# A planned kernel of two attentions: V projected in three parts, VectorE's scores in a third bank, and new planner settings

## The chip, the cores and the metric

The kernel runs on one core of a Trainium2 chip. The engines of the core work side by side and wait for each other by semaphores: TensorE (PE in the profile, PEld for its weight loads), VectorE (DVE), ScalarE (ACT), GpSimd (POOL) and SyncE (SP), which issues nearly all transfers here. The metric is the device time of one execution in microseconds; lower is better.

## The reference

Two attentions over the same input `x` (2048 tokens, 640 features, bf16), mixed by a gate per token:

```python
x = A_x
g = _sigmoid((x * gate_w).sum(-1, keepdims=True))
a = _A_ref(x, A_wqkv, A_wo)
b = _B_ref(x, B_wqkv, B_wo)
return g * a + (1 - g) * b
```

Both have 32 heads of 20 features. A is full softmax attention, every query with all 2048 keys:

```python
scores = jnp.einsum("bhqd,bhkd->bhqk", q, k) * scale
p = _softmax(scores, axis=-1)
o = jnp.einsum("bhqk,bhkd->bhqd", p, v)
return (...)(o).reshape(B, S, D) @ wo
```

B lets each query see 8 keys, at the distances 0, 2, ... 14 before it (positions before the start are masked), with the same softmax, sum over V and output projection.

## The kernel before

**Tiling.** A's work is cut into 32 groups: 4 blocks of 512 queries (`qc`) by 8 sets of 4 heads (`q`), in the order of `GROUPS`. A group has 64 units: 16 blocks of 128 keys (`kb`) by 4 heads (`j`). A unit is one matmul of scores, 128 keys by 512 queries, with the 20 features of a head in one quarter of the array's rows, so up to four units of different `j` run at once. Its exponential and a matmul with V (21 columns: a column of ones gives the sum of the softmax) follow; the four heads of a group accumulate in the four column quarters of `obank`.

**Two ways to the exponential.** Most units go through ScalarE: a tile is two or three units whose scores fill two or three PSUM banks of `score[s % 2]`, and one ACTIVATE (L1652) takes 1024 or 1536 columns to bf16 in `ebuf`. Other units go through VectorE in quads (one `kb`, four `j`). Such a unit "rides" with a tile: its scores are written by the same score matmuls (`qk`, L1616 to L1647), and VectorE turns them into bf16 bit patterns with an add and a max (L1642, into `uD`). Each quad is then used four times with shifted exponents (L866 adds the shift, GpSimd scales V in L857, and the sums go into `obank` in L1693).

**Banks.** Three PSUM banks are shared: `side[0]` is a bank of its own, and `side[1]` and `side[2]` are the third banks of the two score buffers. Side work takes them: the projections of Q, K and V (`mm_group`, L577, matmuls on L592), the gate, B's attention and the output projections. A tile can have three units, or two and a ride, only if the third bank `x` of its own score buffer is free; otherwise it has two units.

**Order.** The order of all engines is fixed when the program is built. A planner keeps a clock for each engine, adds a charge for every task (`T`), and works through the tiles. `next_tile` (L1577) picks the units and asks `wanted` (L1505) for a ride; `qk`, `exp` and `pv_slot` place scores, exponential and sums; then `spend` lets side work run until a limit, the planned end of the exponential before plus `SLACK`. Side work is a set of generators with priorities. A generator yields what it wants next: `("bank", need)` for a shared bank, `("pe", charge, ready)`, `("dve", ...)`, or `("cond",)` and `("cond2", time)` to wait; `step` (L1226) decides whether it gets it. PE works strictly in the planned order, so a matmul that waits holds up all later ones, scores too. `filler` (L1700, matmuls on L1714) adds matmuls whose result isn't used where the planned load of PE is below `FILL`.

**Settings.** `PLAN` (L50) holds a tuple of 21 settings per entry and the tile number from which it holds: slacks, tolerances for a bank that is nearly free (`XTOL`), priorities, limits on VectorE's lag and on quads, and others (list on L1806).

**Projections.** `gen_v(half)` (L762) projects V in two halves of 320 columns, that is 16 heads: a block of 128 tokens in one bank, 20 column-tiled matmuls, one copy by VectorE (L773) into `vA`. The first block of the first half is `v_first` and `v_out` (L1372, L1380), before the first scores; the other fifteen follow from the start (priority 1), and the second half begins with the second group. `gen_kd` (L620) projects K in five chunks, the next when the group in `KPACE` is reached. `gen_qd` (L689) projects Q per chunk and query block (bank, matmuls, copy to `dst` in L706), moves it into `qT` with DMAs (L709), takes absolute values (L715), multiplies by `KMd` in a further bank (L729; this gives a bound for the exponent), and sends the bound, `qbnd`, into `qT` too (L749). B's weights are rearranged by 15 copies on GpSimd (L884, `gen_bweights`). `gen_b` has small matmuls of 64 columns (L996 and L1006) in its middle.

Of the kernel before, what the change touches and what calls it, by code (L numbers as in the profile page):

```python
# [14 lines left out]
P = 128  # L15
# [20 lines left out]
POS = {c: g for g, c in enumerate(GROUPS)}  # L36

# [13 lines left out]
    0: ((0.3, 0.64), 0.39, 2.5, 2.5, 0.49, -1.3, -0.1, 11.8, 7.0, 7.2, 0.49, 0.47, 4.4, 4.0, 0.0, 0.75, 2, -3, 0.36, 4.0, 3.0),  # L51
    10: ((0.3, 0.64), 0.32, 2.5, 2.5, 0.45, -1.3, -0.1, 13.26, 7.0, 7.2, 0.49, 0.68, 4.4, 4.0, 0.0, 0.6, 2, 0.0, 0.5, 4.0, 4.0),
    20: ((0.3, 0.64), 0.32, 2.5, 2.5, 0.45, -1.3, -0.1, 13.26, 7.0, 7.2, 0.35, 0.68, 4.4, 4.0, 0.0, 0.6, 2, 0.0, 0.5, 4.0, 3.0),
    30: ((0.3, 0.49), 0.54, 2.5, 2.5, 0.45, -1.26, -0.1, 13.26, 6.2, 7.2, 0.35, 0.68, 4.4, 4.23, 0.0, 0.6, 2, 0.0, 0.5, 4.0, 3.0),
    40: ((0.3, 0.49), 0.54, 2.5, 2.5, 0.45, -1.32, -0.1, 13.26, 6.2, 7.2, 0.35, 0.66, 4.4, 4.23, 0.0, 0.6, 2, 0.0, 0.5, 4.0, 2.0),
    50: ((0.3, 0.52), 0.54, 2.5, 2.5, 0.67, -1.26, -0.28, 13.26, 6.2, 8.47, 0.35, 0.68, 4.4, 4.23, 0.0, 0.71, 2, -3, 0.5, 4.0, 3.0),
    70: ((0.35, 0.49), 0.54, 2.5, 2.5, 0.97, -1.6, -0.28, 12.22, 6.2, 7.47, 0.17, 0.7, 3.98, 3.89, -0.1, 0.7, 2, -3, 0.5, 4.0, 3.0),
    80: ((0.35, 0.49), 0.54, 2.5, 2.5, 0.97, -1.6, -0.28, 12.22, 6.2, 7.47, 0.17, 0.7, 3.98, 3.89, -0.08, 0.7, 2, -3, 0.5, 4.0, 3.0),
    90: ((0.35, 0.49), 0.54, 2.5, 2.5, 0.97, -1.09, -0.28, 12.22, 6.2, 7.47, 0.17, 0.7, 3.98, 3.89, -0.08, 0.63, 2, -3, 0.5, 4.0, 3.0),
    100: ((0.41, 0.49), 0.61, 2.5, 2.5, 1.07, -1.09, -0.28, 11.68, 6.2, 7.47, 0.17, 0.7, 2.76, 3.89, -0.08, 0.59, 2, -3, 0.5, 4.0, 4.0),  # L60
    110: ((0.32, 0.49), 0.5, 2.5, 2.5, 0.92, -0.82, -0.28, 15.02, 6.2, 9.99, 0.17, 0.7, 2.14, 3.89, -0.08, 0.68, 2, -3, 0.44, 4.0, 4.0),
    120: ((0.28, 0.49), 0.54, 2.5, 2.5, 0.97, -1.6, -0.28, 12.22, 6.2, 7.47, 0.17, 0.7, 3.98, 3.71, -0.03, 0.7, 2, -3, 0.5, 4.0, 3.0),
    140: ((0.32, 0.49), 0.5, 2.5, 2.5, 0.92, -0.82, -0.28, 15.02, 6.2, 9.99, 0.19, 0.7, 2.14, 3.89, -0.08, 0.68, 2, -3, 0.44, 4.0, 4.0),
    150: ((0.32, 0.49), 0.5, 2.5, 2.5, 0.92, -0.71, -0.28, 15.73, 6.2, 10.9, 0.19, 0.64, 2.14, 3.89, 0.02, 0.68, 2, -3, 0.44, 4.0, 4.0),
    170: ((0.3, 0.64), 0.32, 6.6, 2.5, 0.49, -1.3, -0.1, 9.4, 7.0, 7.2, 0.52, 0.47, 4.46, 4.0, 0.0, 0.9, 2, 0.0, 0.5, 4.0, 3.0),
    180: ((0.3, 0.64), 0.32, 6.6, 2.5, 0.66, -1.3, -0.1, 9.4, 7.0, 7.2, 0.52, 0.47, 4.46, 4.0, 0.0, 0.9, 2, 0.0, 0.5, 4.0, 3.0),
    190: ((0.3, 0.64), 0.32, 6.6, 2.5, 0.66, -1.3, -0.1, 9.4, 4.5, 7.2, 0.52, 0.47, 4.46, 4.0, 0.0, 0.9, 2, 0.0, 0.5, 4.0, 3.0),
    200: ((0.3, 0.64), 0.32, 6.6, 2.5, 0.66, -1.3, -0.1, 9.4, 5.5, 7.2, 0.52, 0.48, 4.46, 4.0, 0.0, 0.9, 2, 0.0, 0.5, 4.0, 3.0),
    210: ((0.3, 0.64), 0.32, 6.6, 2.5, 0.63, -1.6, -0.1, 9.4, 5.5, 7.2, 0.5, 0.48, 4.35, 4.0, 0.0, 0.88, 2, 0.0, 0.5, 4.0, 3.0),
    220: ((0.3, 0.64), 0.32, 6.6, 2.5, 0.49, -1.3, -0.1, 11.8, 7.0, 7.2, 0.48, 0.47, 4.4, 4.0, 0.0, 0.6, 2, 0.0, 0.5, 4.0, 3.0),  # L70
    230: ((0.28, 0.49), 0.54, 2.5, 1.0, 0.97, -1.6, -0.28, 12.22, 6.2, 7.47, 0.17, 0.7, 3.98, 3.34, 0.04, 0.7, 2, -3, 0.5, 4.0, 3.0),
    240: ((0.3, 0.47), 0.54, 2.5, 2.5, 0.67, -1.26, -0.28, 13.26, 6.2, 8.47, 0.35, 0.68, 4.4, 4.23, 0.0, 0.71, 2, -3, 0.5, 4.0, 3.0),
    250: ((0.3, 0.47), 0.54, 2.5, 2.5, 0.67, -1.26, -0.28, 13.26, 6.2, 8.47, 0.35, 0.68, 4.4, 4.23, 0.0, 0.71, 2, -3, 0.41, 4.0, 3.0),
    260: ((0.3, 0.47), 0.54, 2.5, 2.5, 0.67, -1.26, -0.28, 13.26, 6.2, 8.47, 0.39, 0.68, 4.4, 4.23, 0.0, 0.71, 2, -3, 0.17, 4.0, 3.0),
    270: ((0.3, 0.55), 0.54, 2.5, 2.5, 0.67, -1.26, -0.23, 13.26, 6.7, 8.77, 0.39, 0.72, 4.4, 4.23, -0.17, 0.71, 2, -3, 0.17, 4.0, 3.0),
    280: ((0.3, 0.64), 0.32, 6.6, 2.5, 0.49, -1.5, -0.1, 11.8, 1.0, 7.2, 0.48, 0.47, 4.4, 4.0, 0.0, 0.6, 2, 0.0, 0.5, 4.0, 3.0),
    290: ((0.3, 0.64), 0.28, 6.6, 6.6, 0.49, -1.5, -0.1, 11.8, 6.7, 7.2, 0.48, 0.46, 4.4, 4.0, 0.0, 0.6, 2, 0.0, 0.5, 4.0, 3.0),
    300: ((0.3, 0.47), 0.54, 2.5, 2.5, 0.6, -1.05, -0.28, 12.11, 6.2, 8.47, 0.39, 0.62, 4.4, 4.23, 0.0, 0.71, 1, -3, 0.17, 4.0, 3.0),
    310: ((0.3, 0.38), 0.54, 2.5, 2.5, 0.6, -1.05, -0.28, 12.11, 6.2, 8.47, 0.39, 0.62, 4.4, 4.23, 0.0, 0.71, 1, -3, 0.17, 4.0, 3.0),
    340: ((0.25, 0.64), 0.32, 6.6, 2.5, 0.66, -1.3, -0.06, 10.84, 4.5, 5.62, 0.52, 0.7, 4.46, 3.26, 0.0, 0.9, 2, 1, 0.52, 4.0, 3.0),  # L80
    350: ((0.3, 0.64), 0.23, 5.5, 2.5, 0.71, -1.07, -0.1, 8.63, 4.5, 7.2, 0.52, 0.48, 4.21, 4.0, 0.0, 0.9, 2, 0.0, 0.35, 4.0, 3.0),
    360: ((0.3, 0.64), 0.23, 6.6, 2.5, 0.71, -1.07, -0.1, 8.63, 4.5, 7.2, 0.52, 0.48, 4.21, 4.0, 0.0, 0.9, 2, 0.0, 0.35, 4.0, 2.0),
    380: ((0.3, 0.64), 0.23, 6.6, 2.5, 0.71, -1.07, -0.1, 8.63, 4.5, 7.2, 0.61, 0.48, 4.21, 4.0, 0.0, 0.9, 2, 0.0, 0.35, 4.0, 2.0),
    390: ((0.3, 0.64), 0.23, 6.6, 2.5, 0.71, -1.07, -0.1, 8.63, 4.5, 7.2, 0.61, 0.48, 4.21, 4.0, 0.0, 0.73, 2, 0.0, 0.35, 4.0, 2.0),
    400: ((0.3, 0.64), 0.23, 6.6, 2.5, 0.71, -1.07, -0.1, 8.63, 4.5, 7.2, 0.61, 0.48, 4.61, 4.0, 0.0, 0.7, 2, 0.0, 0.35, 4.0, 2.0),
    410: ((0.3, 0.64), 0.23, 6.6, 2.5, 0.6, -1.07, -0.1, 8.63, 4.5, 7.2, 0.61, 0.48, 4.61, 4.0, 0.07, 0.7, 2, 0.0, 0.35, 4.0, 2.0),
# [1803 lines left out]
```

## Time and profile before

| | us |
|---|---|
| median of 3 runs | 802.85 (802.61 to 802.86) |
| profiled execution, its time | 802.24 |
| its span, first to last instruction | 800.4 |
| TensorE busy in it | 770.4 |
| ScalarE busy | 779.5 |
| VectorE busy | 717.6 |
| GpSimd busy | 143.6 |
| DMA, mean rate over the span | 44 GB/s |

The granted TensorE clock was 1.00 throughout. "Busy" joins the times in which at least one instruction of an engine is under way. For TensorE the ends are modelled, and consecutive ACTIVATEs overlap at their ends. So the text goes by the distance between starts where it asks what an instruction costs. In rows of the timeline the first number is the start, the second how long the merged instructions took together, and the bracket at the end is the idle time of the engine before them and what ended it. In a row of a group, the two numbers after the bar are the busy time in us and the mean of one instruction in ns.

### The profile page before, as it was taken

The numbers are of one execution on the slowest core, as the hardware profiler recorded it, in microseconds if no ns is written. First come the engines' busy times: TensorE is split into PE (matmuls) and PEld (weight loads), VectorE is DVE, ScalarE is ACT, GpSimd is POOL, SyncE is SP. The second block draws the span as 40 slices with busy tenths as digits, with TensorE's granted clock in tenths as the row PEclk, the third lists the DMA queues.
The fourth block names the chain that finished last, engine by engine and source line by source line (L and its number), as shares of the span: only waits on it lengthen the run. The fifth ranks groups of instructions, "written<-read, shape, count | busy, mean of one in ns | idle before, by whom it ended". The sixth has DMA issues, their size and how long they took to land.

```text
span 800.4 us, 29142 instructions
## 1 busy us (share of the span) xinstructions
PE 770.4 (96%) x12193; PEld 274.6 (34%) x12194; DVE 717.6 (90%) x1291; ACT 779.5 (97%) x785; POOL 143.6 (18%) x239
## 2 busy tenths in 40 slices
PE   9999999999999999999999999999999999999997
PEld 5332223233333333432333334233333233333232
DVE  7567989999879999899989979999999988999995
ACT  5999999999999999999999999999999999999996
POOL 5004111105511211111111111111112111211110
PEclk9999999999999999999999999999999999999999
DMA  9101101012111301300122023022003001303001
GB/s 310 48 16 38 34 18 41 11 33 65 32 36 27 82 20 27 71 16 22 38 70 43 9 50 69 17 61 51 14 22 79 16 26 41 76 6 71 14 7 36
DMA packets 59446, 35.24 MB, mean 44 GB/s; under 512 B 25252, under 2 KB 58116, under 8 KB 59316
## 3 DMA queue, kind: packets, MB, share of 16 engines
q1 hardware_dynamic: 59028, 33.05, 16.7%
q8 instruction: 97, 1.59, 0.9%
q14 instruction: 33, 0.27, 0.1%
q10 hardware_dynamic: 288, 0.33, 0.1%
HBM read 11.45 MB, written 2.62 MB: 18 GB/s over the span
## 4 chain that ended last, share of the span: by engine, by line
PE 50%; ACT 30%; issue 12%; DVE 7%; ACTq 0%; DVEq 0%
ACT ebuf L1652 30%; PE score L1629 17%; PE obank L1693 14%; PE side L592 9%; PE score L592 4%; DVE uD L1642 3%; DVE uD L866 1%; PE side L1714 1%; PE obank L1714 1%; PE score L1321 1%; PE obank L493 1%; PE side L1050 1%; DVE stage L1036 0%; PE score L1714 0%; PE side L954 0%
## 5 line engine op out<-in xcount | busy, mean ns | idle before, releaser
L1652 ACT ACTIVATE ebuf<-score 128x1024 bf16<-128x1024 f32 (+1 forms) x750 | 766.9, 1192 | 4.7 <-PE score L1629 3.6
L1629 PE MATMUL score<-qT,kT 32*128 32x512 bf16 x2048 | 304.6, 384 | 21.3 <-ACT ebuf L1652 15.8
L1642 DVE TENSOR_SCALAR uD<-score 128x512 int16<-128x512 f32 x380 | 254.0, 680 | 23.7 <-PE score L1629 22.3
L866 DVE TENSOR_SCALAR uD<-uD 128x2048 int16<-128x2048 int16 x285 | 195.0, 701 | 7.0 <-PE obank L1693 6.3
L1629 PEld LDWEIGHTS score<-qT,kT 32*128 32x128 bf16 x2048 | 73.3, 91 | 275.7 <-ACT ebuf L1652 214.1
L1693 PE MATMUL obank<-ebuf,vA 128*21 128x512 bf16 x1668 | 164.8, 386 | 0.3 <-DVE oTt L806 0.2
L857 POOL TENSOR_TENSOR vS<-vA,vw 128x252 bf16<-128x252 bf16 x95 | 58.2, 613 | 472.1 <-DVE uD L866 320.4
L1693 PE MATMUL obank<-uD,vS 128*21 128x512 bf16 x1140 | 100.3, 380 | 0.0
L592 PE MATMUL side<-xT,kvw 128*32 128x256 bf16 (+1 forms) x1830 | 78.8, 284 | 0.2 <-DVE rQ L1015 0.2
L1693 PEld LDWEIGHTS obank<-ebuf,vA 128*21 128x21 bf16 x1668 | 40.8, 88 | 98.9 <-issue 77.7
L592 PEld LDWEIGHTS side<-xT,kvw 128*32 128x32 bf16 x1830 | 43.9, 96 | 29.1 <-issue 13.7
L1036 DVE TENSOR_TENSOR stage<-stage,eB 128x1280 bf16<-128x1280 bf16 x64 | 51.1, 815 | 0.0
L938 DVE TENSOR_TENSOR stage<-qkvB 128x1280 bf16<-128x1280 bf16 x64 | 50.9, 815 | 0.1
L824 POOL TENSOR_TENSOR oN<-oTt,rcp 128x256 bf16<-128x256 f32 (+1 forms) x61 | 38.4, 644 | 46.5 <-DVE uD L866 21.8
L592 PE MATMUL score<-xT,kvw 128*32 128x256 bf16 (+1 forms) x930 | 44.3, 296 | 0.0
L1693 PE MATMUL obank<-uD,vA 128*21 128x512 bf16 x380 | 35.3, 379 | 0.0
L922 DVE CAST qkvB<-side 128x512 bf16<-128x512 f32 (+1 forms) x51 | 29.2, 582 | 1.7 <-PE side L592 1.6
L1693 PEld LDWEIGHTS obank<-uD,vS 128*21 128x21 bf16 x1140 | 26.9, 90 | 11.1 <-issue 3.6
L592 PE MATMUL side<-woBp,oB 128*32 128x512 bf16 (+1 forms) x520 | 27.8, 308 | 0.5 <-DVE oB L1061 0.5
L592 PE MATMUL side<-woA_d,oTd 128*32 128x512 bf16 (+1 forms) x472 | 27.2, 310 | 0.0
L806 DVE STREAM_TRANSPOSE oTt<-obank 128x512 f32<-128x512 f32 x32 | 22.7, 708 | 4.4 <-PE obank L1693 4.3
L592 PEld LDWEIGHTS score<-xT,kvw 128*32 128x32 bf16 x930 | 21.0, 95 | 15.3 <-issue 10.7
(202 smaller groups left out, 542.6 us busy)
## 6 DMA issues: line engine op xcount, KB each, us to landing
stage<-qkvB SPq DMA_DIRECT2D x128, 82.5 KB, 2.2
stage<-in_B_wqkv_dram SPq DMA_DIRECT2D x1, 2400.0 KB
oTd<-oN SPq DMA_DIRECT2D x108, 20.0 KB
WqP<-in_A_wqkv_dram SPq DMA_DIRECT2D x13, 160.0 KB, 2.5
qT<-dst SPq DMA_DIRECT2D x104, 20.0 KB
out_dram<-outsb SPq DMA_DIRECT2D x12, 160.0 KB
kvw<-in_A_wqkv_dram SPq DMA_DIRECT2D x2, 800.0 KB
qT<-qbnd SPq DMA_DIRECT2D x72, 1.0 KB
```

The source lines that it names most:

```text
L592: ins = e.matmul(o[j:k, :], l(j) if callable(l) else l[:, j:k], r, start=(first and i == 0), stop=(last and i == n - 1), skip_group_check= ...
L806: T("dve", 0.623, lambda e: e.transpose(oTt[:, :], obank[:, :]), reads=["obank"], writes=["oTt"])
L824: T(en, c2 if half < 0 else 0.56, lambda e: e.tensor_tensor(oo, ii, ib, ALU.mult), reads=["rcp", "oTt"], writes=[("oN0", h) for h in ((0, ...
L857: T("pool", 0.62, lambda e: e.tensor_tensor(vS[:, d % NVS, :, :], _ap(vA, (kb * NQ + q) * 4 * DV, [[0, K - 1], [1, 4 * DV]]), _ap(vw, 0, [ ...
L866: T("dve", 0.066 + 0.1334 * n, lambda e, k=k: e.tensor_scalar(uD[u][:, 0:512 * n].bitcast(I16), uD[u][:, 0:512 * n].bitcast(I16), SHIFTS[k ...
L922: t = TB(dvc(n * TOK), lambda e, o=o, i=i: e.tensor_copy(o, i), reads=[("side", b)], writes=[key])
L938: TB(dvc(CN * TOK, 2), lambda e, w=w, ks=ks: e.tensor_tensor(prodB(w), qB[:, :, :], ks, ALU.mult), reads=["qB", "kB"], writes=[("prod", w) ...
L1036: TB(dvc(CN * TOK, 2), lambda e, o=o, vs=vs, ee=ee: e.tensor_tensor(o, vs, ee, ALU.mult), reads=["eB", ("prod", k)], writes=[("prod", k + ...
L1629: ins = e.matmul(o, kT[32 * j:32 * j + 32, q, kb * P:(kb + 1) * P], qT[g % NQT][32 * j:32 * j + 32, :], start=True, stop=True)
L1642: t = T("dve", 0.6, lambda e: e.tensor_scalar(uD[d % NU][:, 512 * i:512 * (i + 1)].bitcast(I16), side[x], UOFF, 0.0, op0=ALU.add, op1=ALU. ...
L1652: exps[s] = T("act", actc(512 * n), lambda e: e.activation(ebuf[s % NE][:, 0:512 * n], score[s % 2][:, 0:512 * n], ACTF.Exp, scale=LN2 / S ...
L1693: ins = e.matmul(obank[32 * j:32 * j + DV, :], v, src, start=(kb == 0), stop=(last and k >= len(lst) - 4), skip_group_check=True)
```

## The change

The file has new line numbers after it; L592 becomes L591, L729 becomes L730, L866 becomes L879, L884 becomes L897, L1629 becomes L1659, L1642 becomes L1672, L1652 becomes L1682, L1693 becomes L1723 and L1714 becomes L1744.

- V is projected in three parts: 4 heads (80 columns), 12 (240) and 16 (320). A bank takes six blocks of the first part (four in `v_first`), two of the second, one of the third, with one copy for each bank. `VP(q)` tells which part a head set needs. The second part is a generator of its own with priority 1.3; the third starts where the second half started.
- A tile may give its ride the bank `side[0]` (`rbank = 0`): a tile of two that couldn't have its third bank, and, where the new setting `RSIDE` is over 0.5, a tile of three, which then has four score matmuls. `waiting0` refuses it while another shared bank is in use and side work asks for one.
- `gen_qd` asks for its banks only when weights and input are there and `dst` is nearly free, and when `qbnd` is free for the second one.
- The charges of the small matmuls are lower: 0.12 to 0.058 for four of 128 columns (L730), 0.12 to 0.032 and 0.24 to 0.062 for those of 64 in `gen_b`.
- `KPACE` is (0, 2, 4, 5, 6) instead of (0, 1, 3, 5, 6), `D0`, the first time of a quad, 22 instead of 26, and `PLAN` is new in all entries, each with 22 settings.

```diff
+VP = lambda q: 0 if q == 0 else 1 if q < 4 else 2
 PLAN = {
-    0: ((0.3, 0.64), 0.39, 2.5, 2.5, 0.49, -1.3, -0.1, 11.8, 7.0, 7.2, 0.49, 0.47, 4.4, 4.0, 0.0, 0.75, 2, -3, 0.36, 4.0, 3.0),
...
+    0: ((0.26, 0.64), 0.32, 2.5, 2.5, 0.49, -1.3, -0.1, 11.8, 7.0, 7.2, 0.48, 0.47, 4.12, 4.0, -0.14, 0.75, 2, 0.0, 0.5, 4.0, 3.0, 1.0),
...
-    xheld = [None]
+    xheld = [None, None]
+    rbanks = []
-    KPACE = (0, 1, 3, 5, 6)
+    KPACE = (0, 2, 4, 5, 6)
...
+                yield ("cond2", max(sch.ready(*WQ, *XT(qc)), sch.free(("dst", nd_[0] % ND)) - 1.5))
                 b = yield from bank()
...
+                yield ("cond2", sch.free("qbnd"))
                 yield ("pe", 0.0, sch.ready(qk_) - 0.2)
                 b = yield from bank(.12)
-                yield ("pe", 0.12 * len(fl), sch.ready(qk_))
+                yield ("pe", 0.058 * len(fl), sch.ready(qk_))
...
-    def gen_v(half):
-        for kb in range(NV0 if half == 0 else 0, KBN):
-            while half and g1 < 2 + VPACE * kb / KBN:
+    VC0, VCN = (0, 80, 320), (80, 240, 320)
+    def v_mms(o, kb, part):
+        c0, n = VC0[part], VCN[part]
+        return [(o, xT[:, c, kb * P:(kb + 1) * P], kvw[:, WV_OFF + c * D + c0:WV_OFF + c * D + c0 + n]) for c in range(CN)]
+    def v_copy(b, kb, m, part):
+        n = VCN[part] // DH
+        o = _ap(vA, (kb * NQ * 4 + VC0[part] // DH) * DV + 1, [[NQ * 4 * DV, m], [DV, n], [1, DH]])
+        i = sap(b, 0, [[VCN[part], m], [DH, n], [1, DH]])
+        t = T("dve", dvc(m * VCN[part]), lambda e: e.tensor_copy(o, i), reads=[("side", b), "vAones"],
+              writes=[("vA", k, part) for k in range(kb, kb + m)])
...
+    def gen_v(part):
+        m = (6, 2, 1)[part]
+        for kb in range(4 if part == 0 else 0, KBN, m):
+            while part == 2 and g1 < 2 + VPACE * kb / KBN:
                 yield ("cond",)
             b = yield from bank()
+            for i in range(m):
+                yield from mm_group(b, v_mms(side[b][:, i * VCN[part]:(i + 1) * VCN[part]], kb + i, part), ["WvA"] + XT((kb + i) // 4),
+                                    mmc(VCN[part]), per=5 if part == 0 else 2 if part == 1 else 1)
             yield ("dve",)
+            release(b, v_copy(b, kb, m, part))
...
-            yield ("pe", 0.12, sch.ready("gwT", *XT(qc)))
+            yield ("pe", 0.032, sch.ready("gwT", *XT(qc)))
...
-        yield ("pe", 0.24, sch.ready("eB", "Rep"))
+        yield ("pe", 0.062, sch.ready("eB", "Rep"))
...
-                if not bank_used[b] and b != xheld[0] and (best is None or max(bank_free[b], now) < max(bank_free[best], now)):
+                if not bank_used[b] and b not in xheld and (best is None or max(bank_free[b], now) < max(bank_free[best], now)):
...
     def v_first():
         def fn(e):
-            for c in range(CN):
-                ins = e.matmul(side[0][:, 0:320], xT[:, c, 0:P], kvw[:, WV_OFF + c * D:WV_OFF + c * D + 320],
-                               start=(c == 0), stop=(c == CN - 1))
+            for kb in range(4):
+                for c, (o, l, r) in enumerate(v_mms(side[0][:, 80 * kb:80 * kb + 80], kb, 0)):
+                    for j in range(0, P, 32):
+                        ins = e.matmul(o[j:j + 32, :], l[:, j:j + 32], r, start=(c == 0), stop=(c == CN - 1), skip_group_check=True)
             return ins
...
+    add_gen(gen_v(1), 1.3)
...
-    D0 = 26.0
+    D0 = 22.0
...
-            if len(us) == 2 and not ride:
-                ride = wanted([j for j in range(4) if all(uu % 4 != j for uu in us)])
-                if ride:
-                    break
+            if len(us) == 2 and not ride and n == 3:
+                if RSIDE > 0.5 and not bank_used[0] and bank_free[0] <= now + XTOL and not waiting0():
+                    ride = wanted([j for j in range(4) if all(uu % 4 != j for uu in us)])
+                    if ride:
+                        rbank = 0
+                if not ride:
+                    ride = wanted([j for j in range(4) if all(uu % 4 != j for uu in us)])
+                    if ride:
+                        break
             us.append(g * 64 + lo)
             ahead[g][0] += 1
+        if not ride and len(us) == 2 and n == 2 and not bank_used[0] and bank_free[0] <= now + XTOL and not waiting0():
+            ride = wanted([j for j in range(4) if all(uu % 4 != j for uu in us)])
+            if ride:
+                rbank = 0
...
+        xheld[0] = x if ride and rbank == x or len(us) == 3 else None
+        xheld[1] = 0 if ride and rbank == 0 else None
...
+    def waiting0():
+        return sum(bank_used) >= 1 and any(ent[3][0] == "bank" for ent in gens)
```

62 lines of the change are left out of this document (28 added, 34 removed), and 117 rows, old and new, of the table PLAN.

## The prediction

> **What bounds the kernel now.** I read four views of the profile in this order: the busy table of the page, the chain of waits, the groups by form, and the timeline around single waits. The first two, from the page:
>
> ```profile
> PE 770.4 (96%) x12193; PEld 274.6 (34%) x12194; DVE 717.6 (90%) x1291; ACT 779.5 (97%) x785; POOL 143.6 (18%) x239
> ...
> PE 50%; ACT 30%; issue 12%; DVE 7%; ACTq 0%; DVEq 0%
> ACT ebuf L1652 30%; PE score L1629 17%; PE obank L1693 14%; PE side L592 9%; PE score L592 4%; DVE uD L1642 3%; DVE uD L866 1%; PE side L1714 1%; PE obank L1714 1%; PE score L1321 1%; PE obank L493 1%; PE side L1050 1%; DVE stage L1036 0%; PE score L1714 0%; PE side L954 0%
> ```
>
> ScalarE and TensorE are both full, and the chain goes to and fro between them: scores (L1629), exponential (L1652), then the next scores into the bank that the exponential has left. A busy PE counts modelled ends, so I need its real load, and ACT's exponentials overlap, so I need their distance from start to start. Rows of the timeline give both: first stretches in which exponentials of one width follow each other, then a stretch of PE.
>
> ```profile
> 80.52 10.16 ACT L1652 ACTIVATE ebuf<-score 128x1024 bf16<-128x1024 f32 x11
> 89.56 1.12 ACT L1652 ACTIVATE ebuf<-score 128x1024 bf16<-128x1024 f32 x1
> 491.44 8.16 ACT L1652 ACTIVATE ebuf<-score 128x1536 bf16<-128x1536 f32 x6
> 496.77 2.84 ACT L1652 ACTIVATE ebuf<-score 128x1536 bf16<-128x1536 f32 x2
> ...
> 284.73 0.39 PE L1629 MATMUL score<-qT,kT 32*128 32x512 bf16 x2
> 285.05 0.40 PE L1693 MATMUL obank<-ebuf,vA 128*21 128x512 bf16 x4
> 285.27 0.39 PE L592 MATMUL score<-xT,WqP 128*32 128x512 bf16 x4
> 285.59 0.60 PE L1629 MATMUL score<-qT,kT 32*128 32x512 bf16 x3
> 286.12 0.29 PE L592 MATMUL side<-xT,kvw 128*32 128x256 bf16 x4
> ```
>
> The eleventh narrow exponential starts at 89.56, so one costs (89.56 - 80.52)/10 = 0.904 us. The fifth wide one starts at 496.77: (496.77 - 491.44)/4 = 1.332. On PE four column-tiled matmuls of 512 columns cost 285.27 - 285.05 = 0.22. A pass of scores (row-tiled, two or three together) costs 285.05 - 284.73 = 0.32, the same 0.22 and 0.10 for the change of tiling; the change back is in 285.59 - 285.27 = 0.32. Where two score blocks of a tile share rows of the array, they run in two passes (285.59 to 286.12, 0.53).
>
> **ACT's time taken apart.** The first exponential starts at 18.46, the last (one of 512 columns) at 791.47, so the stretch between is 773.0. The 580 exponentials of 1024 and 169 of 1536 take 580 x 0.904 + 169 x 1.332 = 749.4; the small activations among them (8 of 512 columns, 8 of 64, 4 of 16, at 0.48, 0.10 and 0.12 from start to start) take 5.1. The rest, 18.5 us, is exponentials that started late. Two of these are large:
>
> ```profile
> 20.80 0.48 DVE L773 CAST vA<-score 128x320 bf16<-128x320 f32 x1
> 21.33 0.60 PE L1629 MATMUL score<-qT,kT 32*128 32x512 bf16 x5 [1.05 <-DVE vA L773]
> 21.77 1.45 ACT L1652 ACTIVATE ebuf<-score 128x1536 bf16<-128x1536 f32 x1 [1.86 <-PE score L1629]
> ...
> 65.01 5.89 POOL L884 COPY kvw<-stage 128x640 bf16<-128x640 bf16 x4
> 68.24 1.41 DVE L715 TENSOR_SCALAR outsb<-dst 128x512 uint16<-128x512 uint16 x1
> 69.70 0.24 PE L729 MATMUL side<-outsb,KMd 128*32 128x128 bf16 x4 [1.19 <-DVE outsb L715]
> 70.30 2.37 ACT L1652 ACTIVATE ebuf<-score 128x1024 bf16<-128x1024 f32 x2 [1.09 <-PE score L1629]
> ```
>
> At 21.77 the second tile is late by 21.77 - 18.46 - 1.33 = 1.98, because its third bank still held V until VectorE had copied it. At 70.30 the loss is 1.25 (by the starts in the trace): an L715 that takes 0.28 in the median took 1.41 beside GpSimd's weight copies, PE waited for it in L729, and the next scores stood behind L729. The other 15.3 us are spread: by the starts in the trace nearly all are under 0.3 each, the late scores standing right behind PE work without a pause. So in the steady part the limit is ACT's throughput, plus the tiles for which PE comes a little late.
>
> **The change, part by part.** The order of the built program shows what the planner made of all edits together; I price that order, since the new table cannot be priced line by line.
>
> (1) *Fewer, wider exponentials.* 511 of 1024 columns and 215 of 1536 in place of 580 and 169; the one of 512 stays, and VectorE still takes 380 score blocks. So 69 x 0.904 = 62.4 goes and 46 x 1.332 = 61.3 comes: **-1.1 us** on ACT, which nothing hides. [...]
>
> (2) *TensorE.* Over the built order, from the first scores to the last, I add 0.216 for each four concurrent matmuls of 512 columns (in proportion for others) and 0.105 for each change of tiling. Before: 727.5 us of work in 773.0. After: 709.3. The difference of -18.2 is 84 fewer changes of tiling (-8.8), 23 fewer score passes and some fewer double ones (-7.5), 44 fewer filler matmuls of L1714 (-2.4), and +0.5 elsewhere. V in three parts streams the same columns, 640 in each of 16 blocks, and 64-column matmuls, the nearest to the new 80, run at 0.03 for four (L996), so the narrow parts cost nothing extra. What lighter PE is worth: I took the 20 us windows from 80 to 780. The eight in which PE was busy under 19.1 us (18.80 on average) hold 0.25 us of late starts each, the eight over 19.8 (19.95) hold 0.51, so 0.22 us for each us of PE work. That gives -18.2 x 0.22 = -4.0 as one end. The other end: the smaller charges take 8 x (5 x 0.088 + 0.178) = 4.9 and 36 x 0.062 = 2.2 out of the planner's clock, which were hidden reserve; if all 7.1 are filled, 7.1 x 0.22 = +1.6. As the planner places side work up to nearly the same limits (0.3 for tiles of two), I take half of the gain, **-2.0**.
>
> (3) *The start.* VectorE's copy that the second tile waits for grows from 320 to 480 columns; by L773 (0.488) and the 512-column copies of L922 (0.68) it takes 0.65, so **+0.2** at 21.77. The rest of V's early work moves after that point, and K's first chunk comes forward.
>
> (4) *VectorE and the queues.* 27 copies of V in place of 32, about 0.7 us of VectorE's 717.6, is not on the path. POOL has as many instructions, SP as many transfers. Taking Q's banks later could delay qT. Counting the work of ACT between the KMd matmuls (L729) and the first scores of their group, before had 10.7, 10.3 and 9.9 us for the three tightest of the early groups, with no wait on these transfers in the chain; after has 14.3, 12.5 and 10.3. I cost it at nothing; if the cover went, each late group would wait on part of a landing.
>
> (5) *The wait at 70.30.* It needs a stretched VectorE instruction in front of L729; that can return elsewhere or not: -1.25 to +1.25, taken as 0. The tail after the last exponential (800.4 - 792.2 = 8.2 us) has the same instructions: 0.
>
> Sum: -1.1 - 2.0 + 0.2 = **-2.9**. The profiled execution took 802.24 (span 800.4), so 799.3 with a span of 797.5; the median 802.85 is 0.6 above it, which gives **799.9**.
>
> **Rivals.** (A) *The freed PE time is refilled*, late starts stay at 18.5: only -1.1 + 0.2 = -0.9, 801.9. For it: spread lateness comes from where side work is put, and freed PE time is the planner's to fill. Against: ACT's chain leaves PE 772 - 709 = 63 us spare instead of 45.
>
> (B) *Late starts follow PE's load in full* and the wait at 70.30 is gone: -1.1 - 4.0 + 0.2 - 1.25 = -6.1, 796.7. For it: the windows above. Against: their slope rests on eight windows a side.
>
> (C) *GpSimd's copies of B's weights hold up VectorE in front of the KMd matmuls more often.* L884 has 15 copies of 1.35 to 1.46 us; eight L866 and one L715 were stretched beside GpSimd work (to 0.96 to 1.85), and one of these nine reached the path, for 1.25. After, VectorE starts its score blocks earlier (15 instead of 7 in the first 40 us of exponentials), so it is denser where the first copies run; the copies are now broken up by other GpSimd work. With five new waits the sum is -2.9 + 6.25 = +3.3, 806.2; it makes the kernel slower by over 0.2% from four on (+2.1, 804.9). [...]
>
> (D) *The edits don't do what they say.* Only 25 of 380 score blocks go to the side bank in the built order, but the 727 tiles are there whoever caused them, so this changes no time.
>
> **How the numbers follow.** Forecast 0.43, (B) 0.26, (A) 0.14, (C) 0.17, (D) none of its own. A measurement of this kernel tells 0.2%, 1.6 us, from no change. Forecast (nearly all) and (B) are faster, (A) is the same, (C) slower: 0.68, 0.15, 0.17. The forecast's own range, with part (2) from -4.0 to 0, is 797.9 to 801.9. The range for 8 in 10 takes in most of (B) and (C) up to three new waits (+0.9, 803.7): 795.5 to 804.0.
>
> **What would show it.** Right: pitches of 0.904 and 1.332 again, first exponential near 18.5, the second tile 2.1 late, and late starts of 16 to 17 us in all with PE's gaps grown. Late starts of 18 with more side work right before late scores mean (A); 13 or less mean (B). Further rows of over a microsecond in which L730 or the scores wait on a stretched VectorE instruction, beside the weight copies (L897), mean (C). A first exponential or a tail off by over 0.5 us, or a score that waits on a qT transfer, would make the sum wrong in a place I put at nothing.

## The result, and the profile after

| | before | after |
|---|---|---|
| median of 6 runs, us | 802.86 (802.61 to 803.82) | 807.25 (806.03 to 809.62) |
| ratio, 95% interval | | 1.0059 (1.0041 to 1.0077) |
| profiled execution, its time | 802.24 | 807.63 |
| its span | 800.38 | 805.83 |

The change made the kernel slower by 4.4 us; the forecast was 2.9 us faster, with a range that ended at 804.0. The page of the profile after, first the busy table, then the instruction queue of the DMA table, then the chain of waits:

```profile
PE 759.5 (94%) x12485; PEld 279.4 (35%) x12485; DVE 713.9 (89%) x1286; ACT 777.7 (97%) x762; POOL 140.3 (17%) x239
...
q8 instruction: 99, 1.62, 0.8%
...
ACT 45%; PE 33%; issue 18%; DVE 2%; DMA 1%; SPq 0%; ACTq 0%; DVEq 0%
```

TensorE is busy 10.9 us less, as meant, and its share of the chain fell from 50% to 33%. "Issue" grew from 12% to 18%: time in which an engine waited for nothing that the profile shows. These shares don't say where 5.5 us of span went. For that I take ACT's time apart as in the prediction: the start of the first exponential, the floor (exponentials and small activations back to back), the late starts by stretch of the span, and what follows the start of the last exponential. All in us; the columns e1 and e8 are two of the experiments below.

| | before | after | e1_full | e8_parts |
|---|---|---|---|---|
| first exponential | 18.46 | 19.35 | 18.59 | 19.69 |
| floor | 754.97 | 753.75 | 753.75 | 753.75 |
| late, up to 40 us | 2.02 | 8.52 | 2.11 | 2.10 |
| late, 60 to 80 | 1.71 | 0.23 | 0.24 | 0.24 |
| late, 180 to 220 | 1.19 | 2.26 | 2.22 | 0.53 |
| late, all the rest | 13.11 | 12.84 | 13.05 | 12.91 |
| from the last start to the end | 8.91 | 8.88 | 8.88 | 8.87 |

The first row differs between executions: kernels with before's program up to there had 18.46, 19.01, 18.74 and 20.16 in their profiles. Neither the 0.89 of after nor any other difference in this row is therefore put down to the change; where profiles are compared below, it is by late starts. The loss stands in one row: +6.50 in the first 40 us. The timeline of after there (start, duration, engine, line, operation, tiles, shape, count, and in brackets the idle time before it with what ended it):

```profile
18.08 0.90 PE L1390 MATMUL side<-kvw,xT 128*32 128x80 bf16 x80
18.91 0.39 PE L1659 MATMUL score<-qT,kT 32*128 32x512 bf16 x3
19.23 0.32 PE L591 MATMUL score<-kvw,xT 128*32 128x80 bf16 x13
19.35 1.45 ACT L1682 ACTIVATE ebuf<-score 128x1536 bf16<-128x1536 f32 x1 [0.65 <-PE score L1659]
21.26 1.85 PE L591 MATMUL score<-kvw,xT 128*32 128x80 bf16 x107 [1.71 <-issue]
...
25.53 1.19 PE L591 MATMUL side<-kvw,xT 128*32 128x80 bf16 x59 [2.08 <-issue]
26.66 1.03 PE L1659 MATMUL score<-qT,kT 32*128 32x512 bf16 x5
27.31 2.36 ACT L1682 ACTIVATE ebuf<-score 128x1536 bf16<-128x1536 f32 x2 [6.51 <-PE score L1659]
...
28.26 2.34 PE L591 MATMUL score<-xT,WqP 128*32 128x512 bf16 x20
...
31.19 2.59 ACT L1682 ACTIVATE ebuf<-score 128x1536 bf16<-128x1536 f32 x2 [1.52 <-PE score L1659]
```

TensorE stops twice in the middle of V's narrow matmuls, 1.71 and 2.08 us, and no semaphore explains it. ScalarE waits 6.51 us for its second tile. Counted over TensorE's matmuls, weight loads and semaphore instructions from the program's start, 448 and 704 come before the two stops (440 and 696 matmuls and weight loads, and 8 semaphore instructions), 256 apart. The trace of the instruction queue (q8) shows 99 transfers of 16 KB. TensorE has 25,455 instructions in the trace, 257 for each transfer, so I take one transfer to be a block of 256. Those that begin at 18.87 and 22.93 are followed by the first instruction after each stop 2.4 and 2.6 us later. Eighty narrow matmuls and their loads pass in 0.90 us (first row), so 256 instructions are used up in some 1.4 us (an estimate), less than these 2.4 and 2.6. Rows of the same stretch in windows of 2 us (length, busy time and count of TensorE, its weight loads, VectorE, ScalarE and GpSimd, then the granted clock, DMA share and rate in GB/s):

```profile
18.00:20.00 2.00, 1.55 (x98) 1.05 (x96) 1.46 (x3) 1.35 (x3) 2.00 (x3) 1.00 1.03 409
20.00:22.00 2.00, 0.74 (x56) 0.74 (x60) 1.80 (x3) 0.80 (x1) 1.42 (x2) 0.86 1.01 405
22.00:24.00 2.00, 1.45 (x88) 1.26 (x76) 0.81 (x3) 0.00 (x0) 0.00 (x0) 0.50 0.21 79
...
30.00:32.00 2.00, 2.00 (x23) 0.49 (x19) 0.69 (x1) 0.81 (x1) 0.00 (x0) 0.58 0.17 26
32.00:34.00 2.00, 2.00 (x28) 0.42 (x20) 1.24 (x3) 1.88 (x3) 0.00 (x0) 1.00 0.30 64
```

The granted clock is 0.5 from 21.45, 0.2 us after the first stop has ended, to 31.69, for 10.2 us; Q's 20 matmuls at 28.26 take 2.34 us where e1_full's took 1.26. It was 1.00 in every window of before. The other thing to see is the load: until 22 us the DMA engines are full (share 1.0, some 405 GB/s) with the 2.4 MB of B's weights, and the instruction queue's transfers are counted on the same 16 engines (q8's 0.8% above is a share of them).

### The profile page after: what moved, and what is told of

Same layout as the page of the kernel before. It is cut to its first block, busy times and chain, and to the rows that moved or that the text cites. A ratio compares the mean times of both kernels' runs of the same rounds, so it can differ in the third digit from the quotient of the medians.

```text
span 805.8 us, 29670 instructions
## 1 busy us (share of the span) xinstructions
PE 759.5 (94%) x12485; PEld 279.4 (35%) x12485; DVE 713.9 (89%) x1286; ACT 777.7 (97%) x762; POOL 140.3 (17%) x239
## 3 DMA queue, kind: packets, MB, share of 16 engines
q1 hardware_dynamic: 59028, 33.05, 16.6%
## 4 chain that ended last, share of the span: by engine, by line
ACT 45%; PE 33%; issue 18%; DVE 2%; DMA 1%; SPq 0%; ACTq 0%; DVEq 0%
ACT ebuf L1682 44%; PE score L1659 11%; PE obank L1723 9%; PE side L591 6%; PE score L591 4%; DMA oB<-in_A_x_dram 1%; DVE uD L1672 1%; PE obank L1744 1%; PE side L967 0%; DVE uD L879 0%; PE side L1744 0%; PE score L1334 0%; PE score L1744 0%; ACT eB L998 0%; PE score L967 0%
## 5 line engine op out<-in xcount | busy, mean ns | idle before, releaser
L1682 ACT ACTIVATE ebuf<-score 128x1024 bf16<-128x1024 f32 (+1 forms) x727 | 765.2, 1237 | 11.2 <-PE score L1659 10.4
L1659 PE MATMUL score<-qT,kT 32*128 32x512 bf16 x2023 | 292.4, 385 | 32.0 <-ACT ebuf L1682 23.2
L1672 DVE TENSOR_SCALAR uD<-score 128x512 int16<-128x512 f32 x355 | 237.8, 682 | 17.7 <-PE score L1659 16.5
L879 DVE TENSOR_SCALAR uD<-uD 128x2048 int16<-128x2048 int16 x285 | 192.9, 694 | 10.6 <-PE obank L1723 9.9
L1659 PEld LDWEIGHTS score<-qT,kT 32*128 32x128 bf16 x2023 | 71.3, 91 | 278.5 <-ACT ebuf L1682 211.7
L1723 PE MATMUL obank<-ebuf,vA 128*21 128x512 bf16 x1668 | 165.3, 387 | 0.8 <-DVE uD L879 0.7
L1723 PE MATMUL obank<-uD,vS 128*21 128x512 bf16 x1140 | 100.4, 379 | 0.0
L591 PE MATMUL side<-xT,kvw 128*32 128x256 bf16 (+1 forms) x2000 | 85.6, 287 | 0.9 <-DVE oB L633 0.5
L1723 PEld LDWEIGHTS obank<-ebuf,vA 128*21 128x21 bf16 x1668 | 40.9, 89 | 99.9 <-issue 77.9
L591 PEld LDWEIGHTS side<-xT,kvw 128*32 128x32 bf16 x2000 | 47.8, 96 | 29.3 <-issue 15.4
L591 PE MATMUL score<-xT,kvw 128*32 128x256 bf16 (+2 forms) x760 | 34.8, 291 | 0.3 <-DVE uD L1672 0.3
L1723 PE MATMUL obank<-uD,vA 128*21 128x512 bf16 x380 | 34.3, 379 | 0.0
L1723 PEld LDWEIGHTS obank<-uD,vS 128*21 128x21 bf16 x1140 | 27.5, 91 | 9.3 <-issue 2.9
L591 PE MATMUL side<-kvw,xT 128*32 128x320 bf16 (+2 forms) x680 | 25.7, 283 | 2.1 <-issue 2.1
L829 POOL TENSOR_TENSOR rcp<-rcp,gA 128x16 f32<-128x16 f32 x31 | 6.9, 222 | 115.4 <-DVE rcp L823 40.5
L591 PE MATMUL side<-woBp,oB 128*32 128x128 bf16 (+1 forms) x520 | 24.6, 294 | 0.3 <-DVE oB L1074 0.2
```

The lines of the kernel that those rows point to most:

```text
L591: ins = e.matmul(o[j:k, :], l(j) if callable(l) else l[:, j:k], r, start=(first and i == 0), stop=(last and i == n - 1), skip_group_check= ...
L879: T("dve", 0.066 + 0.1334 * n, lambda e, k=k: e.tensor_scalar(uD[u][:, 0:512 * n].bitcast(I16), uD[u][:, 0:512 * n].bitcast(I16), SHIFTS[k ...
L1659: ins = e.matmul(o, kT[32 * j:32 * j + 32, q, kb * P:(kb + 1) * P], qT[g % NQT][32 * j:32 * j + 32, :], start=True, stop=True)
L1672: t = T("dve", 0.6, lambda e: e.tensor_scalar(uD[d % NU][:, 512 * i:512 * (i + 1)].bitcast(I16), side[y], UOFF, 0.0, op0=ALU.add, op1=ALU. ...
L1682: exps[s] = T("act", actc(512 * n), lambda e: e.activation(ebuf[s % NE][:, 0:512 * n], score[s % 2][:, 0:512 * n], ACTF.Exp, scale=LN2 / S ...
L1723: ins = e.matmul(obank[32 * j:32 * j + DV, :], v, src, start=(kb == 0), stop=(last and k >= len(lst) - 4), skip_group_check=True)
```

## The experiments

Each run is compared with the kernel before on the same chip, whose medians there were 803.25 (e1 to e4), 803.00 (e5 to e8) and 803.01 (e9 to e11).

**The start.** The theory (S in the expectations): narrow matmuls outrun the supply of instructions. One rival (T): the load of B's weights holds up the start, be it the operands or the supply of instructions. The other (C): the loss lies in the steady part, with its new order of banks, rides and table.

e1_full computes V's first part with full-array matmuls of 80 columns, five where there were twenty; the orders of all other engines stay.

```diff
-                    for j in range(0, P, 32):
-                        ins = e.matmul(o[j:j + 32, :], l[:, j:j + 32], r, start=(c == 0), stop=(c == CN - 1), skip_group_check=True)
+                    ins = e.matmul(o, l, r, start=(c == 0), stop=(c == CN - 1), skip_group_check=True)
...
-                                    mmc(VCN[part]), per=5 if part == 0 else 2 if part == 1 else 1)
+                                    mmc(VCN[part]), per=5 if part == 0 else 2 if part == 1 else 1, w=P if part == 0 else 32)
```

> The changed kernel with V's first part in full-array matmuls of 128x80: a quarter of the instructions for the same columns (80 instead of 320 in all), every engine's order else unchanged. Theory S (PE's instructions come in blocks of 256, and the 80-column quarters use a block up in some 1.2 us while the next needs 2.4 to 2.6 us): the pauses put down to issue near 19 and 23 us go, the clock stays at 1.00, the second tile is 2 to 3 us late instead of 6.6, and the median falls by 5 to 8 us to 799 to 802. Rival T (the start is slow for its data: the load of B's weights takes the transfers' time and V's or K's operands come late): the pauses stay where they are, 805 to 809. Rival C (the steady part is worse, the start hardly matters): at most 2 us faster.

Measured: 801.77 (800.64 to 806.27), ratio to before 0.9987 (0.9974 to 1.0001). The timeline of e1_full:

```profile
18.48 1.25 PE L591 MATMUL score<-kvw,xT 128*128 128x80 bf16 x30
19.56 0.88 PE L591 MATMUL side<-kvw,xT 128*128 128x80 bf16 x20
20.89 0.64 DVE L773 CAST vA<-score 128x480 bf16<-128x480 f32 x1
21.59 0.60 PE L1658 MATMUL score<-qT,kT 32*128 32x512 bf16 x5 [1.15 <-DVE vA L773]
22.03 5.54 ACT L1681 ACTIVATE ebuf<-score 128x1536 bf16<-128x1536 f32 x5 [1.99 <-PE score L1658]
...
22.59 1.26 PE L591 MATMUL score<-xT,WqP 128*32 128x512 bf16 x20
```

No stop, clock 1.00, and the second tile is late by 22.03 - 18.59 - 1.33 = 2.11, the 2.1 of the prediction's part (3). 240 matmuls and as many weight loads less, with the same order and the load in its old place, take away all of the loss. So it isn't the steady part, and operands that come late because of the load aren't the cause either.

e3_bload leaves V as it is in after and issues the load of B's weights later, once Q of the second group is projected; the other queues keep their order.

```diff
+        T("sp", 10.0, lambda e: e.dma_start(_ap(stage, 0, [[3 * D, CN], [1, 3 * D]]), wB_v[:, :, :]), writes=["stage", ("xs", 3)], dma=True, iss=2.0)
...
-    T("sp", 10.0, lambda e: e.dma_start(_ap(stage, 0, [[3 * D, CN], [1, 3 * D]]), wB_v[:, :, :]), writes=["stage", ("xs", 3)], dma=True, iss=2.0)
```

> The changed kernel with the 2.4 MB load of B's weights issued after the second group's Q instead of before the first tile; all other queues in the same order. Theory S, blocks fetched at their own pace: the two pauses stay, shorter by at most 0.5 us each, 805 to 808. Rival T (the load holds up the start, be it operands or the fetch of instructions): the pauses shrink to under 1 us in all, 799 to 803.

Measured: 802.80 (802.20 to 804.39), ratio 0.9994 (0.9984 to 1.0003). Its timeline:

```profile
19.44 1.26 PE L591 MATMUL score<-kvw,xT 128*32 128x80 bf16 x120
...
22.73 0.72 PE L591 MATMUL side<-kvw,xT 128*32 128x80 bf16 x59 [1.82 <-issue]
23.38 0.60 PE L1659 MATMUL score<-qT,kT 32*128 32x512 bf16 x5
23.82 3.71 ACT L1682 ACTIVATE ebuf<-score 128x1536 bf16<-128x1536 f32 x3 [2.81 <-PE score L1659]
...
26.46 0.39 PE L1723 MATMUL obank<-ebuf,vA 128*21 128x512 bf16 x3 [0.28 <-issue]
```

The time lies where the rival (the load holds up the start) had put it, not at the 805 to 808 of theory S; the stops are more than that rival allowed. The one at 448 is gone: its block's transfer began at 16.14, with TensorE at instruction 232 (18.87 and 417 in after). The one at 704 stays (1.82 us), and a short one at 960 (26.46) comes, both without a drop of the clock. The late starts up to 40 us are 3.41: against e1_full's 2.11 the stop at 704 makes the second tile 0.8 later, and the one at 960 a later tile 0.5. The other 5.1 of after's 8.52 go with its first stop and the halved clock; how they divide was not separated. So the load and the matmuls' number are both needed for the whole of after's loss.

How the load does it is open. From a transfer's begin to the first instruction after its stop it is 2.4 us beside the full load (after, 18.87) and 2.6 without it (here, 20.11), so the load doesn't lengthen this time. What may differ is when the transfer begins: with the load in its old place, the block behind instruction 448 began to arrive between 15.28 and 19.87 in the profiles of eleven kernels, without it at 16.14 and 16.78 (here and in e5_both).

e2_split is the converse on the kernel before: blocks 1 and 2 of V's first half in four pieces of 80 columns each.

```diff
+            if half == 0 and kb in (1, 2):
+                mms = [(o[:, i * 80:(i + 1) * 80], l, r[:, i * 80:(i + 1) * 80]) for o, l, r in mms for i in range(4)]
+                yield from mm_group(b, mms, ["WvA"] + XT(kb // 4), mmc(320) / 4, per=4)
```

> The kernel before with two of V's blocks (the first two of the generator) in four pieces of 80 columns: 160 instead of 40 matmuls for the same columns, order else unchanged. Theory S: a pause put down to issue appears in them, of 0.5 to 2.5 us, and the kernel gets slower by as much, 803.5 to 806, more if the clock falls too. Rival T and rival C: nothing changes, within 0.5 us of 802.9.

Measured: 802.93, ratio 1.0000 (0.9990 to 1.0009). The time is a miss for the theory, which said 803.5 to 806, and is what the rivals said. The timeline of e2_split shows why:

```profile
21.00 0.83 PE L592 MATMUL side<-xT,WqP 128*32 128x512 bf16 x12 [0.78 <-issue]
21.34 0.48 DVE L777 CAST vA<-score 128x320 bf16<-128x320 f32 x1
...
21.88 0.60 PE L1633 MATMUL score<-qT,kT 32*128 32x512 bf16 x5
```

There is a stop at 448 as in after, now within Q's matmuls, and the scores behind it would have waited for VectorE's copy until about 21.9 in any case. So this stop of 0.78 us is covered. e7_split5 therefore cuts blocks 1 to 5 in the same way (`if half == 0 and kb < 6`), beyond that cover.

> The kernel before with the blocks 1 to 5 of V's first half each in four pieces of 80 columns, 400 small matmuls in place of 100 of 320 columns, the same columns streamed, nothing else of the change in it. Theory (narrow matmuls outrun the fetch of 256 instructions): two or three issue pauses of 1 to 2.5 us at TensorE instruction 448, 704 and perhaps 960 within some 6 us, scores that wait for them, a granted clock of 0.5 for some 10 us, and 805 to 809. Rival (the loss of the changed kernel came with its bank order, rides or table): 803.3 within 0.6.

Measured: 806.26 (804.80 to 806.80), ratio 1.0042 (1.0026 to 1.0057). The timeline of e7_split5:

```profile
27.94 0.39 PE L592 MATMUL side<-kvw,xT 128*32 128x80 bf16 x21 [1.12 <-issue]
...
29.27 2.37 ACT L1656 ACTIVATE ebuf<-score 128x1024 bf16<-128x1024 f32 x2 [1.16 <-PE score L1633]
...
31.40 0.45 PE L592 MATMUL side<-kvw,xT 128*32 128x320 bf16 x6 [0.52 <-issue]
...
32.22 1.45 ACT L1656 ACTIVATE ebuf<-score 128x1536 bf16<-128x1536 f32 x1 [0.58 <-PE score L1633]
```

The kernel before, with nothing of the change but more and narrower matmuls for the same columns, becomes slower by 0.4%. The stops stand at 960 and 1216, again multiples of 256 from 448. The expected ones at 448 and 704 did not come in this execution, in which the block behind 448 began to arrive at 15.69, and the clock stayed at 1.00. Late starts in the first 40 us are 4.40, +2.4; the profiled execution is the quickest of four (804.80), and by the medians the loss is 3.3. So the time is as the theory said, by stops alone and without the expected fall of the clock.

e5_both joins e1_full and e3_bload, to see whether the load does harm by itself.

> The changed kernel with V's first part as full-array matmuls (as in e1_full) and with the load of B's weights issued after Q of the second group (as in e3_bload); orders otherwise as in e1_full. Theory (instruction fetch of TensorE's queue starved at the start): without the narrow matmuls there is no pause left for the later load to shorten, so it stays at e1_full's time, 801.3 to 802.3, second tile 2.1 late. Rival (the load disturbs the start by itself, through the transfers of x): first exponential and second tile come 0.5 to 1 us sooner than in e1_full, 800.8 to 801.3. Against the kernel before, either is 0.9 to 2.0 us faster.

Measured: 801.80, ratio 0.9985 (0.9976 to 0.9994); late starts up to 40 us 2.10 as in e1_full. Without narrow matmuls the place of the load makes no difference, which the theory said.

e4_halves was to undo the three parts alone: the other edits of the change, with V in two halves.

```diff
-VP = lambda q: 0 if q == 0 else 1 if q < 4 else 2
+VP = lambda q: 0 if q < 4 else 2
...
-    VC0, VCN = (0, 80, 320), (80, 240, 320)
+    VC0, VCN = (0, 80, 320), (320, 240, 320)
...
-    add_gen(gen_v(1), 1.3)
```

> The changed kernel with V in two halves of 320 columns, as before the change; side-bank rides, late banks, charges and table stay, the planner orders the rest anew (515 exponentials of 1024 and 215 of 1536: 4 more narrow ones, +3.6 us on ACT). Theory S: no pause put down to issue, the clock stays at 1.00, the start costs what it did before; with the 3.6 us of more exponentials 802 to 806. Rival C: the steady part keeps the loss, 807 to 811.

Measured: 911.68, ratio 1.1352 (1.1334 to 1.1370). This is inconclusive: the planner made another order for the whole kernel from a table that isn't made for it, with single waits of ScalarE of 29 and 32 us near the end where B's work came late. It has no stop at the start, but says nothing of the rest. All other experiments leave the planner's order alone.

**What lighter TensorE is worth.** In e1_full the rest of the late starts is 13.05 against 13.11 before, though TensorE's work is lighter. Two kernels change the load of e1_full without a new plan: e6_load adds 77 groups of four matmuls by a block of zeros into the output bank, e9_light leaves out 84 groups of four PV matmuls (parts of A's sum), both spread evenly.

```diff
+        extra = npv[0] % 9 in (0, 4) and lst[0][1] > 0 and not last
...
+            for j in range(4 if extra else 0):
+                e.matmul(obank[32 * j:32 * j + 32, :], zero[:, :], xT[:, 0, 0:512], start=False, stop=False, skip_group_check=True)
```

> e1_full with 77 groups of four 512-column matmuls by a block of zeros added into the output bank, spread evenly over the tiles, so that TensorE's work grows by 77 x 0.216 = 16.6 us and is nearly that of the kernel before; planner and all orders unchanged. Part (2) of the prediction (0.22 us of late starts for each us of TensorE work, or half of it after refilling): 801.8 + 3.7 = 805.5, and +1.8 at the half. Rival (A) (late starts come from where side work is put, and spare time of TensorE is worth nothing): 801.8 within 0.5, late starts 17.6 within 0.5.

> The mirror of e6_load: e1_full without 84 groups of four PV matmuls of 512 columns, spread evenly over the tiles (these parts of A's sum are left out), so that TensorE's work falls by 84 x 0.216 = 18.1 us below the plan; every wait and order stays. e6_load cost 8 us for 16.6, 0.48 us for each. Theory (late starts follow TensorE's load wherever the placement isn't redone; in the changed kernel the planner had filled the 18 us it gained): 18.1 x 0.2 to 0.48 = -3.7 to -8.7, so 793 to 798, late starts of 9 to 14. Rival (the load counts only above some limit, below it a us of TensorE is worth nothing): 801.0 to 801.8, late starts of 17 or more.

Measured: e6_load 809.81, ratio 1.0084 (1.0070 to 1.0098), late starts 25.90; e9_light 799.74, ratio 0.9955 (0.9944 to 0.9967), late starts 15.51; e1_full has 17.62. So 16.6 us more cost 8.3 in late starts, 0.50 for each, and 18.1 us less gave 2.1, 0.12 for each. Neither run fell where one of its theories had put it: the worth of load isn't one slope, but steeper above the load that the plan counted on than below it. These are two points, and the places where work was added and taken away differ too. e9_light's 2.1 us is what part (2) hoped for; the changed kernel, lighter by as much in its *plan*, has none of it. Its order with before's load (e6_load) has 25.90 us of late starts where before's own order has 18.04. My reading is that the plan places its work closer, and uses up what it was given.

e10_fill takes away load where the planner thought TensorE idle: on e8_parts (below), the 137 groups of filler matmuls shrink from 512 to 64 columns.

```diff
-                ins = e.matmul(o[32 * j:32 * j + 32, :], w[:, 32 * j:32 * j + 32] if best else w[:, :], xT[:, 0, 0:512], start=bool(best),
+                ins = e.matmul(o[32 * j:32 * j + 32, 0:64], w[:, 32 * j:32 * j + 32] if best else w[:, :], xT[:, 0, 0:64], start=bool(best),
```

> e8_parts with its 137 filler groups of four 512-column matmuls cut to 64 columns, so that 137 x (0.216 - 0.03) = 25.5 us of TensorE's work goes at the places where the planner thought TensorE idle; no other instruction moves. Theory (load costs only where the scores stand behind it, and the fillers stand where there was spare time): 799.0 to 800.0, late starts down by under 1.0. Rival (each us is worth what e6_load showed, 0.2 to 0.48): -5 to -12, 788 to 795. If the clock falls without them, over 801.

Measured: 804.05, but from 798.95 to 812.08 over 12 runs, ratio 1.0011 (0.9987 to 1.0035). Windows of e10_fill and then of e8_parts, with the same columns as above:

```profile
720.00:740.00 20.00, 17.62 (x282) 6.25 (x283) 16.35 (x30) 17.94 (x18) 3.23 (x6) 0.75 0.23 52
740.00:760.00 20.00, 17.07 (x192) 4.33 (x184) 16.39 (x27) 16.61 (x18) 2.13 (x5) 0.83 0.13 29
```

```profile
720.00:740.00 20.00, 19.86 (x311) 6.42 (x308) 17.58 (x34) 20.00 (x22) 3.07 (x5) 1.00 0.32 73
740.00:760.00 20.00, 18.48 (x252) 5.56 (x249) 19.84 (x34) 20.00 (x20) 3.29 (x7) 1.00 0.06 13
```

The clock falls to 0.75 and 0.83 in the mean of such windows, and 6.8 us of the late starts of its profile lie in these two. The time of its runs goes with their mean clock (798.95 at 0.998, 804.87 at 0.988, 810.36 at 0.977). By the quickest run the fillers' work is worth 0.7 to 1.1 us at full clock (799.64 is e8_parts' quickest, 800.04 its median); without them the time went with the clock.

**The waits at 180 to 220 us.** After has two late starts of 0.79 and 0.75 us there that before hasn't, e1_full too. The idea was the prediction's (C) in small: a VectorE instruction is held up as long as one GpSimd instruction beside it lasts. e8_parts cuts each of GpSimd's 15 weight copies in e1_full into five.

```diff
-                T("pool", 1.37, lambda e, o=o, i=i: e.tensor_copy(o, i), reads=["stage"],
+                def fn(e, m=m, c=c):
+                    for n in range(CN):
+                        ins = e.tensor_copy(_ap(kvw, (m * CN + c) * D + n * P, [[32, 4], [1, 32]]), _ap(stage, c * 3 * D + m * D + n, [[CN, 4], [DH, 32]]))
+                    return ins
+                T("pool", 1.37, fn, reads=["stage"],
```

> e1_full with each of GpSimd's 15 weight copies of 640 columns (1.34 us) as five of 128 columns (some 0.3 each); no other instruction moves. Theory (rival (C) of the prediction in small: a VectorE instruction is held up as long as one GpSimd instruction beside it lasts): the two waits of 0.79 and 0.73 us between 180 and 220 us go to under 0.3 each, 800.6 to 801.2. Rival (they are held up by the bytes moved, not by the instruction): both waits stay, 801.8 or, with the added overhead of 60 instructions on GpSimd, up to 802.5.

Measured: 800.04 (799.64 to 801.99), ratio 0.9966 (0.9954 to 0.9979). The timeline of e1_full around one of the two waits:

```profile
207.11 3.04 POOL L897 COPY kvw<-stage 128x640 bf16<-128x640 bf16 x2
207.39 1.59 DVE L879 TENSOR_SCALAR uD<-uD 128x2048 int16<-128x2048 int16 x1
208.91 1.27 DVE L1671 TENSOR_SCALAR uD<-score 128x512 int16<-128x512 f32 x2
...
209.73 0.39 PE L1658 MATMUL score<-qT,kT 32*128 32x512 bf16 x3 [0.89 <-ACT ebuf L1681]
...
210.16 3.77 ACT L1681 ACTIVATE ebuf<-score 128x1024 bf16<-128x1024 f32 x4 [0.48 <-PE score L1658]
```

and of e8_parts at the same place:

```profile
207.39 0.68 DVE L879 TENSOR_SCALAR uD<-uD 128x2048 int16<-128x2048 int16 x1
207.44 4.16 POOL L899 COPY kvw<-stage 128x128 bf16<-128x128 bf16 x9
207.60 5.74 ACT L1685 ACTIVATE ebuf<-score 128x1024 bf16<-128x1024 f32 x6
...
207.99 1.28 DVE L1675 TENSOR_SCALAR uD<-score 128x512 int16<-128x512 f32 x2
...
208.81 0.39 PE L1662 MATMUL score<-qT,kT 32*128 32x512 bf16 x3
```

In e1_full the first of the two copies ends at 208.43, and L879 behind it at 208.98. The next VectorE instruction (L1671), which reads scores out of a bank, ends at 209.58, and the scores at 209.73 stand behind TensorE's wait for it (the row names ScalarE, which released 0.1 us later). In e8_parts the same VectorE instruction takes 0.68 in place of 1.59, and the scores start at 208.81, though GpSimd moves the same bytes and needs more time for them (0.41 us for a fifth by itself; the five from 207.10 take 2.29, one stretched to 0.89). ScalarE goes on without a gap, and both waits are gone: 0.53 us of late starts from 180 to 220 for 2.22. The time is somewhat below the 800.6 to 801.2 expected. With this the kernel beats both, before by 0.34%.

e11_bparts makes the same edit in the kernel before, for its wait of 1.25 us at 70 us.

> The kernel before with each of GpSimd's 15 weight copies of 640 columns as five of 128, as in e8_parts; nothing else moves. Theory (a VectorE instruction is held up as long as the one GpSimd instruction beside it): the wait of 1.25 us at 70 us goes, -1.0 to -1.5, 801.5 to 802.0, late starts 16.5 to 17. Rival (held up by the bytes): 802.8 within 0.4, the wait at 70 stays over 0.8.

Measured: 802.41, ratio 0.9989 (0.9980 to 0.9998), late starts 17.09. The L715 that took 1.41 takes 0.50 in e11_bparts:

```profile
69.49 0.50 DVE L715 TENSOR_SCALAR outsb<-dst 128x512 uint16<-128x512 uint16 x1
```

The late starts from 60 to 80 us fall from 1.71 to 0.37; about 0.3 come back between 180 and 220. The gain of 0.6 in the time is less than the 1.0 to 1.5 expected, but has the sign.

## Why the prediction was wrong

**The step that failed** is the sentence of part (2) "V in three parts streams the same columns ... so the narrow parts cost nothing extra", taken from the rate of 64-column matmuls (0.03 for four); part (3) rests on it when it puts the start at +0.2 for a longer copy and nothing else. The rate itself was right (80 matmuls of 80 columns in 0.90 us, 20 of 320 in 0.86). I priced columns and left out that every matmul and every weight load is also an instruction to be fetched. The first part of V is 320 matmuls and as many weight loads, 640 instructions, all between 18.1 and 28.5 us, and up to 22 us beside a load that filled the DMA engines. Put at 0.2 us, the start cost 6.5 in late starts. e1_full shows it by taking the instructions away (6.4 of the 6.5 go), e7_split5 by making stops of the same kind in the kernel before (+2.4, without a fall of the clock), e3_bload that the load beside the narrow matmuls has a share in it.

**Part (1)** was right: the floor fell by 1.22 (-1.1 forecast), with the same distances in both traces (0.904 and 1.33).

**Part (2)** was wrong in its size: -2.0 forecast, and the rest of the late starts fell by 0.27 in after and 0.06 in e1_full. This is rival (A). The slope of the windows (0.22) wasn't absurd, as it lies between the 0.12 and 0.50 measured, but a slope taken at a fixed plan doesn't carry over to a plan that was made with the lower load. Which of the settings or lower charges used it up was not tried alone, since each makes a new order (e4_halves).

**Part (3)** apart from this was right: e1_full's second tile is 2.11 late, as forecast (0.1 more than before).

**Part (4)**: no late start of after over 0.4 us stands behind a qT transfer; nothing as forecast.

**Part (5)** fell as its words allowed, to neither end: the wait at 70.30 went (-1.48 in that stretch), and two stretched VectorE instructions further on brought 1.07 back. Rival (C) had what held VectorE up, GpSimd's copies, and its condition (four waits) wasn't met. (Its "1.35 to 1.46 us" for the 15 copies is a misreading: they took 1.33 to 1.71, and the one beside the L715 of 1.41 took 1.66.) Measured are two instructions: beside GpSimd's fifths the L879 took 0.68 in place of 1.59 (e8_parts), the L715 0.50 in place of 1.41 (e11_bparts); how GpSimd holds VectorE up was not shown.

With part (2) at nothing and part (5) at its measured -0.4 the sum is -1.1 + 0.2 - 0.4 = -1.3; e1_full, which has the start as forecast, is 1.5 below before by the medians (801.77 against 803.25), though the interval of its ratio reaches to 1.0001. The text's own warning, that something at the start would upset a place put at nothing, named the first exponential; it was the second tile.

## What to carry to other kernels

Price a split of matmuls in instructions as well as in columns. Here the 640 instructions at the start, up to 22 us beside a load that filled the DMA engines, were priced at nothing, and the late starts there grew by 6.5 us: 256 instructions were used up in some 1.4 us (an estimate from eighty matmuls and their loads in 0.90), from a transfer's begin to the first instruction after its stop it took 2.4 to 2.6, and the profile shows the stops only as "issue". The plan here spent the time that it was given on TensorE, so measure what lighter load is worth with the order held fixed and again with the new order. Where GpSimd works beside a VectorE that somebody waits for, cut its long instructions into short ones, even if they then take longer in all (in e8_parts five pieces took 2.29 us where one copy had taken 1.32, and the L879 beside them 0.68 in place of 1.59).

## What the runs showed of the hardware

TensorE's instructions arrive in blocks of 256 by three counts, with matmuls, weight loads and semaphore instructions counted alike: after has 99 transfers for 25,455 instructions (257 for each), before 97 for 24,872 (256), and the stops of after, e3_bload and e7_split5 stand at instructions 448, 704, 960 and 1216. At the seven stops at the start of after, e2_split, e3_bload and e7_split5 execution went on 2.4 to 2.6 us after a block's transfer had begun. With eighty narrow matmuls in 0.9 us a block lasts some 1.4 us (an estimate), on average over the span 8 us (99 transfers in 805.8).

The granted clock fell to 0.5 for 10.24 us, 0.2 us behind the first stop of after (1.71 us), but not behind one of 1.82 us with one of 0.28 after it (e3_bload), nor behind two of 1.12 and 0.52, 3.5 us apart (e7_split5). It fell in the steady part of e10_fill when the fillers became short, for 3.41, 3.41, 10.24, 6.83 and 3.41 us: each time a whole number of stretches of 3.41, and so were the 10.24 of after. What decides whether the clock falls was not shown.
